# Running the first feed-forward chunks ahead of attention's last products

## The chip, the cores and the metric

The kernel runs on one core of one Trainium2 chip. The metric is the device time of one execution in microseconds (us). Before the change three runs gave 1016.50, 1019.47 and 1022.62 us, a median of 1019.47.

## What is computed

Three layers stand behind each other. Attention over 4 batches, 8 heads, 576 positions and head size 64 keeps only scores within `tau` of their row's largest. A dense layer `w_in`, `w_out` with a rational function in between (the "feed-forward part" below) takes its result. Last comes a mixture of 8 experts, one for each token.

```python
scores = scale * np.matmul(q, k.transpose(0, 1, 3, 2))
thresh = np.max(scores, axis=-1, keepdims=True) - tau
scores = np.where(scores >= thresh, scores, -1000000000.0)
attn = softmax(scores);  x = attn @ v            # (2304, 512) after the heads are put side by side
h = x @ w_in                                     # (2304, 2048)
g = (a0 + a1 h + a2 h^2 + a3 h^3) / (1 + |b0| |h| + |b1| h^2 + 1e-6)
x = g @ w_out                                    # (2304, 512)
e = argmax(x @ w_gate);  out = gate * sigmoid(x @ w_output_gate)[e] * (relu(x @ w1[e]) @ w2[e])
```

The products are made of two f16 (or rounded f32) parts of each number, a high part and a residue, so that three products stand for one in f32.

## The kernel before

**Attention** goes through 144 steps, one for 128 rows of scores; 18 steps make a pair of heads (group 0 to 7), two steps a pair that shares buffers. In step i TensorE makes the scores of step i + 1 (`emit_s`) and the products with v of step i - 12 (`emit_pv`), VectorE the row's extreme and the mask multiply (`emit_r`, `emit_p`: tiles `mn`, `e`), ScalarE the exponential and the f16 high part (`e`, `php`), GpSimd the residue (`php`, L382 and L388). For each pair SyncE's queue then transposes `php` into `pt`, from which the products with v are made. The scale of ring buffers lets the engines run some pairs ahead of the transposes. Every six steps VectorE normalises the products (`emit_x`: `rinv`, `xf`), which frees the bank for the next six; every eighteen, in three blocks of three token tiles, TensorE transposes x, ScalarE copies the high part into `xT` and VectorE subtracts for the residue (`emit_xt`, `emit_xlo`). The products of the last twelve steps come after step 143.

**The feed-forward part** is a generator, `moe1`, that issues one slot of work at each `next`. Attention calls it from step 112 on, so that slot t goes with step 112 + t; after slot 31 its buffers are opened, and what is behind slot END runs without attention. `w_in` and `w_out` come in 16 pieces each, of 128 columns or rows. The weights are read in 64-bit words, and a piece is decoded: ScalarE makes the exponent (L601), VectorE three operations (L598, L604, L608: `raw`, `mag`, `mag`). A piece of `w_in` is then summed on ScalarE (`sum_in`, L760), the sums of two pieces go through TensorE and VectorE's nine short operations to a scale (`red_in`, `clamp_red`, `scale_in`), and the piece is split: ScalarE scales it and writes the high part `wih` (L807, L808, or L810 for the later ones), GpSimd the residue `wil` (L812). A piece of `w_out` needs no scale (`split_out`: `woh` on ScalarE, `wol` on GpSimd). Pieces stand in the order `STREAM`; `FIRST_AT` gives the slots of the first eight decodes, `DEC_AT` and `DEC_EVERY` those of the others, `IN_LOAD` those of the first loads.

There are 96 **chunks**, each one piece of `w_in` times 384 tokens: twelve products into a bank of `h` (L900). Chunk c is issued in slot START + c, and the products with `w_out` of chunk c five slots later (`acc`, L969). Chunks 0 to 11 are pieces 0 to 3 for the first three blocks of tokens, which stem from head groups 0 to 3 and batches 0 and 1 alone; chunks 28 to 43 are pieces 0 to 15 for the sixth block. Two chunks, a pair, share the rational function. First half: ScalarE `ah`, `s`, `t` (L923 to L925), GpSimd `t` (L926), VectorE `s`, `s` (L928, L929). Second half, one pair later: ScalarE the logarithm and exponential (L935, L936) that give the quotient, VectorE `t`, `h`, `s` (L914 to L916), ScalarE `gh`, GpSimd `gl` (L951). There are two `h` buffers, so that chunk 4 can begin when VectorE has done L916 on pair 0, and chunk 6 when it has on pair 1. Every engine takes its instructions in the order in which they are issued.

Of the kernel before, what the change touches and what calls it, by code (L numbers as in the profile page):

```python
# [9 lines left out]
F32 = mybir.dt.float32  # L10
# [119 lines left out]
SUM_AT = (0, 1, 1, 2, 2)  # L130


def attention(nc, tc, q, k, v, tau, xT, vs, ident, tail):

# [6 lines left out]
    def pool(c, name, bufs, **kw):  # L141
        return c.enter_context(tc.tile_pool(name=name, bufs=bufs, side="right", reuse_waits="tile", **kw))
# [3 lines left out]
    pt_p = pool(ctx, "pt", 6)  # L146
    x_p = pool(ctx, "x", 2)
    ps_x = pool(ctx, "ps_x", 1, space=PSUM)
    raw_p = pool(early, "raw", 1)
    t_p = pool(early, "tt", 2)  # L150
    e_p = pool(early, "e", 3)
    ps_s = pool(early, "ps_s", 3, space=PSUM)

    D1 = D + 1
# [16 lines left out]
    tiny = fix.tile([P, P + 6 * D1], BF16, name="tiny")  # L171
    xps = ps_x.tile([P, 6, D1], F32, name="xps")
    xflat = xps.rearrange("p a b -> p (a b)")


    raws = {}
# [310 lines left out]
    def at(step, f, *a):  # L487
        plan.setdefault(step, []).append((f, a))
# [22 lines left out]
    for g in range(1, NG):  # L511
# [20 lines left out]
    pre = {min(6 * n + 6 + LAG, N + LAG - 1): n for n in range(N // 6)}  # L532
    for g in range(NG):
        for tg in range(3):
            s = (g + 1) * GT + PLAN["xt"][tg]
            if g == NG - 1:
                s = min(N + LAG - 1, N + 6 + 6 * tg)
            w = (g + 2, (("kt",), ("qt", 0), ("qt", 1))[tg]) if g + 2 < NG else ()
            at(s, emit_xt, g, tg, *w)
            at(s + 1, emit_xlo, g, tg)  # L540
    emit_s(0)
    i = 0
    while i < N + LAG or plan:
# [11 lines left out]
        if 0 <= i - 1 < N:  # L555
            emit_p(i - 1)
        if i < N:
            emit_thr(i)
        if i in pre and not done:
            emit_x(pre[i])  # L560
        while plan and min(plan) <= i:
            for f, a in plan.pop(min(plan)):
                f(*a)
        if i == N:
            early.close()
        if i >= N - PRE and tail:
            next(tail)
        i += 1
    ctx.close()


# [72 lines left out]
    return ((0, P, b0 + S + t - 5, 4),)  # L644


def moe1(nc, tc, xT, vs, w_in, w_out, a, bb, w_gate, w_ogate, gates, ident, yd, part, L, consts, keep, side):

    ctx, psum = ExitStack(), ExitStack()

# [18 lines left out]
    cvs = d_p.tile([P, 4, 2, NFC], F32, name="cvs")  # L669
    cv = cvs[:, 0]  # L670
    tot = d_p.tile([P, NFC], F32, name="tot")

    wo, ps_b, d2_p = [], [], []

# [62 lines left out]
        return p.tile([P, DM], F32, tag="mag", bufs=n, name="mag")  # L737

    def step(key):
        raw, t = raws[key], mags.pop(key, None)  # L740
        low, high = raw[:, :, 0], raw[:, :, 1]
        out = mags[key] = mag_buf(key[0])
        if t is not None:
            high = t.bitcast(I32)
            t = high
        elif late(key):
            t = aux().bitcast(I32)
            dec.last_bits(raw, t)
            low = t
        else:  # L750
            t = out.bitcast(I32)
            dec.last_bits(raw, low)
        dec.merge(t, high, low)
        dec.sign(out.bitcast(I32), raw[:, :, 1], t)
        del raws[key]
        load_next()

    def sum_in(n):

        nc.scalar.activation(  # L760
            wih[:, :, n * P:(n + 1) * P], mags[0, n].rearrange("p (k f) -> p k f", k=4), AF.Abs,
            accum_out=tot[:, n:n + 1])


# [10 lines left out]

    def red_in(n, m, alone=False):
        if alone:
            sum_rows(h_tile()[:, 0], n, tot[:, n:n + m], m)
        else:
            spare.append(lambda ps: sum_rows(ps, n, tot[:, n:n + m], m))  # L780

# [19 lines left out]
    def split_in(n):  # L801
        f = mags.pop((0, n)).rearrange("p (k f) -> p k f", k=4)
        sc = scales.pop(n)
        hi = wih[:, :, n * P:(n + 1) * P]
        lo = wil[:, :, n * P:(n + 1) * P]
# [14 lines left out]
    at(PRE, coefficients)  # L820
    end = decode_at()
    for key in STREAM:
        t = end[key]
        steps.setdefault(t, []).append(lambda key=key: step(key))
        at(t - SLOT_LEAD[late(key)], exponent, key)
        if late(key) and key[0]:
            at(t - SHIFT_LEAD, last_bits, key)
    n = 0
    for m in GROUPS:
        if n in FIRST_SUMS:  # L830
            t = FIRST_SUMS[n]
# [20 lines left out]
    for n in range(RAW_BUFS):  # L852
        at(IN_LOAD[n], load_next)
    for t in range(PRE):
        for f in chains(t):
            f()
        run(t)
        yield
    c_p = pool("c", 1)
    m_p = pool("m", 1)  # L860
    ps_h = pool("ps_h", 2, space=PSUM)
    ps_a = pool("ps_a", 1, space=PSUM)
    wih = c_p.tile([P, 4, FF], F16, name="wih")
    wil = c_p.tile([P, 4, FF], F16, name="wil")


    chunks = [(j, fc, r) for j, (r, (f0, f1), _) in enumerate(SEGS) for fc in range(f0, f1)]
# [20 lines left out]
    def emit_in(c, fill):  # L888
# [3 lines left out]
        if c < len(chunks):  # L892
            j, fc, r = chunks[c]
            t0 = TR * r
            if not odd:
                hps[p] = h_tile()
            hb = hps[p][:, odd]
            parts = [(wih, k, lo) for k in range(4) for lo in range(2)] + [(wil, k, 0) for k in range(4)]
            for i, (w, k, lo) in enumerate(parts):
                nc.tensor.matmul(  # L900
                    hb[:, 0:n], w[:, k, fc * P:(fc + 1) * P], xT[:, k, t0:t0 + TR, lo, :],
                    start=(i == 0), stop=(i == 11))
# [222 lines left out]
    for t in range(PRE, START + len(chunks) + G_LAG):  # L1125
# [18 lines left out]
        if t in hooks:  # L1144
            run(t)
        if t < END:
            yield
    assert not hooks, hooks
    ctx.close()
# [622 lines left out]
def kernel(ctx, tc, q, k, v, tau, w_in, w_out, a, b, w_gate, w_ogate, w1, w2, out):  # L1772
    nc = tc.nc
    with tc.manual_schedule():
# [20 lines left out]
        xT = mid.tile([P, 4, NTILE, 2, P], F16, name="xT")  # L1795
        masks.make_identity(nc, ident)
        experts = Experts(ctx, nc, tc, yd, L, rt, R, w1, w2, ident, out, xT)
        gen = moe1(nc, tc, xT, vs, w_in, w_out, a, b, w_gate, w_ogate, gates, ident, yd, part, L,
                   lambda tmp: routing_constants(nc, main, tmp, R), ctx, experts)
        attention(nc, tc, q, k, v, tau, xT, vs, ident, gen)  # L1800
        for _ in gen:
            pass
        experts.rest()
# [33 lines left out]
```

## Time and profile before

| | |
|---|---|
| median of three runs | 1019.47 us (1016.5 to 1022.62) |
| the profiled execution | 1021.39 us, of which the span of its instructions is 1019.7 |
| TensorE busy | 932.2 us, 91% of the span |
| VectorE busy | 795.7 us, 78% |
| ScalarE busy | 680.3 us, 67% |
| GpSimd busy | 543.6 us, 53% |
| mean granted clock of TensorE | 0.98 of full |

The busy shares are means over stages with different limits. By the order of time attention fills the span to about 300 us, the feed-forward part with its 96 chunks the stretch to some 755, the experts the rest. The rows below look at the end of attention, the change-over behind it, and the stretch in which the later pieces are decoded beside the chunks.

### The profile page before, as it was taken

The page shows a single profiled execution, that of the slowest core. Times are in us where ns is not written, and L with a number is a line of the kernel's source. Part 1 is how long each engine was busy: PE and PEld are TensorE (multiplying, and loading weights), DVE is VectorE, ACT ScalarE, POOL GpSimd, SP SyncE. Part 2 cuts the span into 40 slices and gives each one's busy share as a digit, 9 for nine tenths or more (in the row PEclk, how much of TensorE's full clock was granted, in tenths as well). Part 3 has the DMA queues.
Part 4 walks back from the last instruction along what each step waited for, and adds up shares of the span by engine and source line. Part 5 has one row for each costly group of instructions (what it writes and reads, how often), then busy time and mean ns, then how long its engine had stood idle before and what let it go on. Part 6 is the DMA issues. An engine that isn't in the chain of part 4 may idle for free.

```text
span 1019.7 us, 20739 instructions
## 1 busy us (share of the span) xinstructions
PE 932.2 (91%) x7899; PEld 683.6 (67%) x7899; DVE 795.7 (78%) x1337; ACT 680.3 (67%) x1006; POOL 543.6 (53%) x540
## 2 busy tenths in 40 slices
PE   8898899999876798999999899998798999999996
PEld 5565566666544465666666666665567899999995
DVE  5898799989896887888768878998983986555652
ACT  5888888888776677887866666656553555455551
POOL 2687689888774588697954344444241132111120
PEclk9999999999998899999999999999899999999998
DMA  9999999999994342232003212041123021111340
GB/s 215 176 208 203 199 190 182 184 196 185 215 196 126 103 143 96 82 114 73 1 1 94 73 53 63 32 106 60 42 52 134 22 63 42 42 42 42 119 130 24
DMA packets 234188, 110.26 MB, mean 108 GB/s; under 512 B 196832, under 2 KB 221408, under 8 KB 234080
## 3 DMA queue, kind: packets, MB, share of 16 engines
q1 hardware_dynamic: 230816, 98.89, 44.9%
q0 software_dynamic: 3120, 9.96, 3.0%
q8 instruction: 64, 1.05, 0.4%
q14 instruction: 44, 0.36, 0.1%
q10 hardware_dynamic: 144, 0.00, 0.0%
HBM read 82.61 MB, written 13.63 MB: 94 GB/s over the span
## 4 chain that ended last, share of the span: by engine, by line
PE 52%; DVE 20%; POOL 9%; issue 7%; ACT 6%; DMA 5%; SPq 0%; POOLq 0%; DVEq 0%; ACTq 0%
PE h L1638 10%; PE o L1655 9%; PE h L900 9%; PE acc L969 7%; PE s L352 5%; PE tp L202 5%; PE xps L410 4%; DMA pt<-php 4%; DVE t L914 2%; DVE h L915 2%; POOL t L926 2%; DVE s L916 2%; DVE s L928 2%; POOL php L382 2%; DVE s L929 2%
## 5 line engine op out<-in xcount | busy, mean ns | idle before, releaser
L382 POOL TENSOR_TENSOR php<-e,php 128x512 f16<-128x512 f32 x144 | 166.3, 1159 | 65.7 <-ACT php L380 65.2
L900 PE MATMUL h<-xT,wih 128*128 128x384 f16 x768 | 147.2, 336 | 37.7 <-DVE s L916 30.5
L926 POOL TENSOR_TENSOR t<-t,ah 128x768 f32<-128x768 f32 x48 | 87.8, 1829 | 167.1 <-ACT t L925 158.3
L900 PEld LDWEIGHTS <-wih 128*128 128x128 f16 x768 | 69.8, 100 | 103.9 <-DVE s L916 40.8
L969 PE MATMUL acc<-woh,gh 128*128 128x512 f32 x288 | 125.7, 437 | 1.1 <-ACT part L986 1.1
L364 ACT ACTIVATE e<-s,mn 128x576 f32<-128x576 f32 x144 | 107.0, 743 | 28.2 <-DVE mn L363 24.9
L376 DVE SCALAR_TENSOR_TENSOR e<-s,mn,e 128x576 f32<-128x576 f32 x144 | 116.4, 808 | 8.8 <-ACT e L364 8.8
L352 PE MATMUL s<-kt,qT 64*128 64x256 f32 (+3 forms) x640 | 115.6, 450 | 7.7 <-DVE mn L369 7.4
L1665 POOL DMA_INDIRECT out_dram<-os,sidx x19 | 23.6, 1243 | 184.3 <-ACT os L1664 154.3
L410 PEld LDWEIGHTS <-pt 128*128 128x128 f16 (+1 forms) x2240 | 78.2, 101 | 59.0 <-issue 55.9
L969 PE MATMUL acc<-woh,gl 128*128 128x512 f32 x288 | 114.0, 396 | 0.3 <-POOL gl L951 0.2
L969 PE MATMUL acc<-wol,gh 128*128 128x512 f32 x288 | 113.9, 396 | 0.0
L363 DVE TENSOR_REDUCE mn<-s 128x1 f32<-128x576 f32 x144 | 107.7, 748 | 6.8 <-PE s L352 6.5
L380 ACT ACTIVATE php<-e 128x576 f16<-128x576 f32 x144 | 98.6, 685 | 12.5 <-DMA pt<-php 11.1
L951 POOL TENSOR_TENSOR gl<-s,gh 128x768 fp32r<-128x768 f32 x48 | 91.4, 1904 | 5.7 <-issue 4.7
L410 PE MATMUL xps<-vs__112,pt 128*128 128x65 f16 (+1 forms) x2240 | 92.5, 195 | 0.0
L935 ACT ACTIVATE h<-t,co 128x768 f32<-128x768 f32 x48 | 43.5, 906 | 69.3 <-POOL t L926 28.6
L900 PE MATMUL h<-xT,wil 128*128 128x384 f16 x384 | 79.9, 332 | 0.0
L914 DVE SCALAR_TENSOR_TENSOR t<-t,co,h 128x768 f32<-128x768 f32 x48 | 48.5, 1011 | 34.7 <-POOL gl L951 22.6
L923 ACT ACTIVATE ah<-h,cvs 128x768 f32<-128x768 f32 x48 | 43.2, 901 | 42.0 <-PE h L900 37.0
L1598 DVE TENSOR_TENSOR wol<-xT,woh 128x1024 fp32r<-128x1024 f32 x45 | 56.8, 1271 | 13.5 <-ACT woh L1597 13.0
L969 PEld LDWEIGHTS acc<-woh,gh 128*128 128x128 f32 x288 | 54.5, 189 | 15.5 <-ACT part L986 2.2
(387 smaller groups left out, 2322.3 us busy)
## 6 DMA issues: line engine op xcount, KB each, us to landing
xT<-in_moe_w_dram SPq DMA_DIRECT2D x80, 512.0 KB
raw<-in_moe_w_in_dram SPq DMA_DIRECT2D x16, 512.0 KB
raw<-in_moe_w_out_dram SPq DMA_DIRECT2D x16, 512.0 KB
yd<-y SPq DMA_DIRECT2D x18, 256.0 KB
raw<-in_k_dram SPq DMA_DIRECT2D x16, 256.0 KB
raw<-in_q_dram SPq DMA_DIRECT2D x16, 256.0 KB
xT<-in_v_dram SPq DMA_DIRECT2D x8, 512.0 KB
part<-part SPq DMA_DIRECT2D x15, 256.0 KB
```

What stands on the lines that cost most here:

```text
L352: nc.tensor.matmul(ps[po:po + m, o:o + n], qT[r, g % 2, hh, t, po:po + m], KT[g][r, bb, c:c + n], start=True, stop=True)
L363: nc.vector.tensor_reduce(mn[:, n:n + 1], st[i], axis=AX.X, op=ALU.min)
L364: nc.scalar.activation(e[:, n], st[i], AF.Exp, bias=mn[:, n:n + 1], scale=-1.0)
L376: nc.vector.scalar_tensor_tensor(e[:, n], st.pop(i), mn[:, 2 + n:3 + n], e[:, n], op0=ALU.is_le, op1=ALU.mult)
L380: nc.scalar.activation(hi, e[:, n], AF.Copy)
L382: nc.gpsimd.tensor_tensor(lo[:, b:b + 512], e[:, n, a:a + 512], hi[:, a:a + 512], op=ALU.subtract)
L410: nc.tensor.matmul(x, pt[:, blk, po:po + m], vv[:, par, hh, j, :], start=False, stop=(i % 6 == 5 and n == 13))
L900: nc.tensor.matmul(hb[:, 0:n], w[:, k, fc * P:(fc + 1) * P], xT[:, k, t0:t0 + TR, lo, :], start=(i == 0), stop=(i == 11))
L926: nc.gpsimd.tensor_tensor(t1, t1, ah, op=ALU.mult)
L969: nc.tensor.matmul(acc[r, i], g[:, i * P:(i + 1) * P], w, start=first and m == 0, stop=last and m == 2)
L1638: self.nc.tensor.matmul(hp[:, a], w[:, k, a], x[:, k], start=(k == 0 and m == 0), stop=(k == K1 - 1 and m == 2))
L1655: self.nc.tensor.matmul(self.Op[j][h], a[:, k, h * P:(h + 1) * P], w[:, k], start=(u == 0 and k == 0 and m == 0), stop=(u == UN - 1 and k ...
```

## The change

Pieces 0 and 1 of `w_in` are decoded and split within attention: the three operations of VectorE on a decode are issued in steps 121, 123, 125 and 127, 129, 131 (`EARLY_STEPS`), the sums in steps 126 and 132, the scale in step 133, the splits in steps 135 and 137. The first four pieces get a buffer of their own, `w4`, that exists from the start, and the buffers for decoded pieces go from 6 to 4 in one pool and from 4 to 6 in the other. The first loads come in steps 112, 115, 125, 129 and 133, not 112, 114, 118, 122 and 127. START goes from 44 to 33, END from 45 to 37, DEC_AT from 48 to 39. After step 143 attention no longer runs its loop on, but calls the generator between its last products: chunks 0 and 1, products of steps 132 to 137, the sums of pieces 2 and 3, products of steps 138 to 141, chunk 2, products of steps 142 and 143, chunk 3, the last two blocks of x.

```diff
-MAG_BUFS = 6
-MAG2_BUFS = 4
+MAG_BUFS = 4
+MAG2_BUFS = 6
-END = 45
-START = 44
+END = 37
+START = 33
-IN_LOAD = (0, 2, 6, 10, 15, 18, 20, 26)
+IN_LOAD = (0, 3, 13, 17, 21, 32, 32)
+EARLY_STEPS = ((9, 11, 13), (15, 17, 19))
+EARLY_SUM = 20
-FIRST_AT = (32, 33, 38, 42, 44, 45, 46, 47)
+FIRST_AT = (13, 19, 32, 33, 35, 37, 37, 38)
-FIRST_SUMS = {0: 41, 2: 43}
-DEC_AT = 48
+SECOND_SUM = 34
+HALVES = (34,)
+DEC_AT = 39
...
+    next(tail)
+    next(tail)
+    for i in range(N - LAG, N - 6):
+        emit_pv(i)
+    next(tail)
+    emit_x(N // 6 - 2)
+    for i in range(N - 6, N - 4):
+        emit_pv(i)
+    next(tail)
+    for i in range(N - 4, N - 2):
+        emit_pv(i)
+    emit_xt(NG - 1, 0)
+    emit_xlo(NG - 1, 0)
+    next(tail)
+    for i in range(N - 2, N):
+        emit_pv(i)
+    emit_x(N // 6 - 1)
+    next(tail)
+    for tg in (1, 2):
+        emit_xt(NG - 1, tg)
...
+    w4 = [d_p.tile([P, 4, 4 * P], F16, name=x) for x in ("wih4", "wil4")]
...
+        if n < 2 * m:
             for i in range(n, n + m):
-                at(end[0, i], sum_in, i)
-                at(t + 1, split_in, i)
-            at(t, red_in, n, m, True)
-            at(t, clamp_red, n, m)
-            at(t, scale_in, n, m)
-            at(t + 2, factors_in, n, m)
+                at(end[0, i] + (n == 0), sum_in, i)
+            t = SECOND_SUM if n else EARLY_SUM + 1
+            at(t + 0.5, red_in, n, m, True)
+            at(t + 0.75, clamp_red, n, m)
+            at(t + 0.75, scale_in, n, m)
+            for i in range(m):
+                at(t + (0.8, 1)[i] if n else t + 2 + 2 * i, split_in, n + i)
+            at(t + 1, factors_in, n, m)
```

GpSimd's list at the end of attention was, from step 134 on (`php`: the residues of a pair of steps):

```order
L333 TENSOR_TENSOR vs__112<-vt,vs__112 128x2x2x64
L382 TENSOR_TENSOR php<-e,php 128x512
L388 TENSOR_TENSOR php<-e,php 128x2x64
L382 TENSOR_TENSOR php<-e,php 128x512 x2
L388 TENSOR_TENSOR php<-e,php 128x2x64
```

and is now, with `cvs` the factors and `wil` the residues of pieces 0 and 1:

```order
L337 TENSOR_TENSOR vs__112<-vt,vs__112 128x2x2x64
L386 TENSOR_TENSOR php<-e,php 128x512
L392 TENSOR_TENSOR php<-e,php 128x2x64
L835 TENSOR_TENSOR cvs<-sc,vs 128x2x2
L838 TENSOR_TENSOR cvs<-cvs 128x2x2
L840 TENSOR_SCALAR cvs<-cvs,co 128x2x2 x2
L386 TENSOR_TENSOR php<-e,php 128x512
L852 TENSOR_TENSOR wil_4009<-mag,wih_4008 128x4x128
L386 TENSOR_TENSOR php<-e,php 128x512
L392 TENSOR_TENSOR php<-e,php 128x2x64
```

Four operations on columns and a residue of a weight piece stand between the residues of attention; a second residue follows in the next pair.

VectorE's list behind attention's last mask multiply was, at its start:

```order
L376 SCALAR_TENSOR_TENSOR e<-s,mn,e 128x576
L598 TENSOR_SCALAR raw<-raw 128x512
L604 SCALAR_TENSOR_TENSOR mag<-raw 128x512
L608 SCALAR_TENSOR_TENSOR mag<-raw,mag 128x512
```

and is now:

```order
L380 SCALAR_TENSOR_TENSOR e<-s,mn,e 128x576
L451 TENSOR_TENSOR xT<-tp,xT 128x3x128
L619 TENSOR_SCALAR raw<-raw 128x512
L625 SCALAR_TENSOR_TENSOR mag<-raw 128x512
L629 SCALAR_TENSOR_TENSOR mag<-raw,mag 128x512
L619 TENSOR_SCALAR raw<-raw 128x512
L625 SCALAR_TENSOR_TENSOR mag<-raw 128x512
L629 SCALAR_TENSOR_TENSOR mag<-raw,mag 128x512
L975 SCALAR_TENSOR_TENSOR s<-s,cvs,h 128x768
L976 SCALAR_TENSOR_TENSOR s<-s,cvs,h 128x768
L424 RECIPROCAL rinv<-xps 128x6
L425 TENSOR_TENSOR xf<-xps,rinv 128x384
```

The decodes are now those of pieces 2 and 3, the first half of chunks 0 and 1 (L975, L976) comes next, and the normalising of steps 132 to 137 behind it.

## Rows read from the trace of the kernel before

**Rows 1.** Busy us by stretch: start:end, length, each engine (instructions), PEclk, DMA share, GB/s.
```profile
255.00:298.00 43.00, 35.20 (x536) 23.12 (x535) 38.34 (x79) 33.99 (x59) 35.50 (x45) 1.00 1.12 203
...
317.38:345.66 28.28, 18.15 (x82) 9.88 (x82) 23.88 (x37) 20.55 (x30) 20.21 (x19) 0.77 0.34 99
345.66:506.72 161.06, 150.75 (x768) 100.33 (x769) 135.24 (x209) 128.53 (x186) 129.42 (x106) 1.00 0.26 84
```

**Rows 2.** SyncE's queue: start, us, queue, line, transfer, count.
```profile
249.23 3.62 SPq L390 DMA_TRANSPOSE pt<-php  x1
...
288.52 18.40 SPq L390 DMA_TRANSPOSE pt<-php  x6
```

**Rows 3.** VectorE's instructions: start, us, line, out<-in; in brackets idling before, releaser.
```profile
263.17 0.82 DVE L376 SCALAR_TENSOR_TENSOR e<-s,mn,e 128x576 f32<-128x576 f32 x1 [2.22 <-ACT e L364]
...
271.59 0.82 DVE L376 SCALAR_TENSOR_TENSOR e<-s,mn,e 128x576 f32<-128x576 f32 x1 [1.40 <-ACT e L364]
...
297.83 0.81 DVE L376 SCALAR_TENSOR_TENSOR e<-s,mn,e 128x576 f32<-128x576 f32 x1
298.55 1.03 DVE L598 TENSOR_SCALAR raw<-raw 128x512 int32<-128x512 int32 x1
...
301.24 0.80 DVE L608 SCALAR_TENSOR_TENSOR mag<-raw,mag 128x512 int32<-128x512 int32 x1
...
302.05 0.42 DVE L598 TENSOR_SCALAR raw<-raw 128x512 int32<-128x512 int32 x1
...
303.30 0.69 DVE L608 SCALAR_TENSOR_TENSOR mag<-raw,mag 128x512 int32<-128x512 int32 x1
...
305.63 0.18 DVE L420 RECIPROCAL rinv<-xps 128x6 f32<-128x6 f32 x1
305.85 0.56 DVE L421 TENSOR_TENSOR xf<-xps,rinv 128x384 f32<-128x384 f32 x1
```

**Rows 4.** TensorE's instructions at the change-over: chunks 4, 6 and 8 begin.
```profile
308.99 2.27 PE L410 MATMUL xps<-vs__112,pt 128*64 128x65 f16 x56
...
334.93 2.74 PE L900 MATMUL h<-xT,wih 128*128 128x384 f16 x8 [8.29 <-DVE s L916]
...
345.66 1.47 PE L900 MATMUL h<-xT,wih 128*128 128x384 f16 x8 [1.84 <-DVE s L916]
...
354.75 1.47 PE L900 MATMUL h<-xT,wih 128*128 128x384 f16 x8 [0.82 <-DVE s L916]
```

**Rows 5.** ScalarE's instructions: copy of x, a split, first half of a pair, logarithm.
```profile
304.66 0.47 ACT L441 ACTIVATE xT<-tp 128x384 f16<-128x384 f32 x1
...
315.27 0.70 ACT L807 ACTIVATE mag<-mag,sc 128x512 f32<-128x512 f32 x1
316.01 0.63 ACT L808 ACTIVATE wih<-mag 128x512 f16<-128x512 f32 x1
...
322.83 0.90 ACT L923 ACTIVATE ah<-h,cvs 128x768 f32<-128x768 f32 x1 [0.50 <-PE h L900]
...
327.46 0.91 ACT L935 ACTIVATE h<-t,co 128x768 f32<-128x768 f32 x1 [0.85 <-POOL t L926]
```

**Rows 6.** VectorE's instructions on pair 0, and a decode between.
```profile
324.65 1.01 DVE L928 SCALAR_TENSOR_TENSOR s<-s,cvs,h 128x768 f32<-128x768 f32 x1 [3.43 <-ACT s L924]
...
326.70 1.01 DVE L598 TENSOR_SCALAR raw<-raw 128x512 int32<-128x512 int32 x1
...
331.81 1.01 DVE L914 SCALAR_TENSOR_TENSOR t<-t,co,h 128x768 f32<-128x768 f32 x1
...
333.85 1.01 DVE L916 SCALAR_TENSOR_TENSOR s<-s,co,h 128x768 f32<-128x768 f32 x1
```

**Rows 7.** TensorE: end of chunk 39, start of chunk 40, and chunk 84.
```profile
495.34 0.81 PE L900 MATMUL h<-xT,wil 128*128 128x384 f16 x4
...
498.34 1.47 PE L900 MATMUL h<-xT,wih 128*128 128x384 f16 x8
...
692.24 2.74 PE L900 MATMUL h<-xT,wih 128*128 128x384 f16 x8 [2.20 <-DVE s L916]
```

**Rows 8.** GpSimd: the residue of piece 14 of w_in.
```profile
503.64 1.16 POOL L812 TENSOR_TENSOR wil<-mag,wih 128x512 f16<-128x512 f32 x1
```

More of the change, by code (lines that the diff above doesn't have):

```diff
@@ L130, with attention @@
 SUM_AT = (0, 1, 1, 2, 2)
-def attention(nc, tc, q, k, v, tau, xT, vs, ident, tail):
+def attention(nc, tc, q, k, v, tau, xT, vs, ident, tail, bank):
     ctx = ExitStack()
@@ L148, in attention @@
     ps_x = pool(ctx, "ps_x", 1, space=PSUM)
+    e_p = pool(early, "e", 3)
+    t_p = pool(early, "tt", 2)
     raw_p = pool(early, "raw", 1)
-    t_p = pool(early, "tt", 2)
-    e_p = pool(early, "e", 3)
     ps_s = pool(early, "ps_s", 3, space=PSUM)
@@ L173, in attention @@
     xflat = xps.rearrange("p a b -> p (a b)")
+    bank.append(lambda: ps_x.tile([P, 4, P], F32, tag="tp", name="tp")[:, 3])
     raws = {}
@@ L531, in attention @@
             at(s0 + s, lo_v, g, a)
-    pre = {min(6 * n + 6 + LAG, N + LAG - 1): n for n in range(N // 6)}
+    pre = {6 * n + 6 + LAG: n for n in range(N // 6 - 2)}
     for g in range(NG):
         for tg in range(3):
-            s = (g + 1) * GT + PLAN["xt"][tg]
+            s = min((g + 1) * GT + PLAN["xt"][tg], N)
             if g == NG - 1:
-                s = min(N + LAG - 1, N + 6 + 6 * tg)
+                continue
             w = (g + 2, (("kt",), ("qt", 0), ("qt", 1))[tg]) if g + 2 < NG else ()
             at(s, emit_xt, g, tg, *w)
-            at(s + 1, emit_xlo, g, tg)
+            at(min(s + 1, N), emit_xlo, g, tg)
     emit_s(0)
-    i = 0
-    while i < N + LAG or plan:
+    for i in range(N + 1):
         if i + 1 < N:
             emit_s(i + 1)
-        done = i in pre and i < N + LAG - 1
-        if done:
+        if i in pre:
             emit_x(pre[i])
-        if 0 <= i - LAG < N:
+        if LAG <= i < N:
             emit_pv(i - LAG)
@@ L554, in attention @@
             emit_r(i)
-        if 0 <= i - 1 < N:
+        if i > 0:
             emit_p(i - 1)
@@ L558, in attention @@
             emit_thr(i)
[L559 to L563, printed above, removed]
+        for f, a in plan.pop(i, ()):
+            f(*a)
         if i == N:
             early.close()
-        if i >= N - PRE and tail:
+        if i >= N - PRE:
             next(tail)
-        i += 1
+    assert not plan, plan
+    next(tail)
[18 more added lines that the diff above has]
+        emit_xt(NG - 1, tg)
+    for tg in (1, 2):
+        emit_xlo(NG - 1, tg)
     ctx.close()
@@ L644, in rows_of, with moe1 @@
     return ((0, P, b0 + S + t - 5, 4),)
-def moe1(nc, tc, xT, vs, w_in, w_out, a, bb, w_gate, w_ogate, gates, ident, yd, part, L, consts, keep, side):
+def moe1(nc, tc, xT, vs, w_in, w_out, a, bb, w_gate, w_ogate, gates, ident, yd, part, L, consts, keep, side, early_bank):
     ctx, psum = ExitStack(), ExitStack()
@@ L739, in step, with step_parts, bits, merge @@
     def step(key):
[L740 to L756, printed above, removed]
+        for part in step_parts(key):
+            part()
+    def step_parts(key):
+        now = {}
+        def bits():
+            raw, t = raws[key], mags.pop(key, None)
+            low, high = raw[:, :, 0], raw[:, :, 1]
+            out = mags[key] = mag_buf(key[0])
+            if t is not None:
+                high = t.bitcast(I32)
+                t = high
+            elif late(key):
+                t = aux().bitcast(I32)
+                dec.last_bits(raw, t)
+                low = t
+            else:
+                t = out.bitcast(I32)
+                dec.last_bits(raw, low)
+            now.update(t=t, high=high, low=low, out=out)
+        def merge():
+            dec.merge(now["t"], now["high"], now["low"])
+        def sign():
+            dec.sign(now["out"].bitcast(I32), raws.pop(key)[:, :, 1], now["t"])
+            if key not in STREAM[:2]:
+                load_next()
+        return bits, merge, sign
     def sum_in(n):
         nc.scalar.activation(
-            wih[:, :, n * P:(n + 1) * P], mags[0, n].rearrange("p (k f) -> p k f", k=4), AF.Abs,
+            w_cols(0, n), mags[0, n].rearrange("p (k f) -> p k f", k=4), AF.Abs,
             accum_out=tot[:, n:n + 1])
@@ L818, in split_out @@
         nc.gpsimd.tensor_tensor(l, f, h.bitcast(F32), op=ALU.subtract)
-    at(PRE, coefficients)
+    at(1, coefficients)
     end = decode_at()
@@ L823, in moe1 @@
         t = end[key]
-        steps.setdefault(t, []).append(lambda key=key: step(key))
+        if key in STREAM[:2]:
+            for x, f in zip(EARLY_STEPS[STREAM.index(key)], step_parts(key)):
+                steps.setdefault(x, []).append(f)
+            t = EARLY_STEPS[STREAM.index(key)][0]
+        else:
+            steps.setdefault(t, []).append(lambda key=key: step(key))
         at(t - SLOT_LEAD[late(key)], exponent, key)
@@ L851, in moe1 @@
     queue = list(STREAM)
-    for n in range(RAW_BUFS):
-        at(IN_LOAD[n], load_next)
+    for t in IN_LOAD:
+        at(t, load_next)
     for t in range(PRE):
@@ L856, in moe1 @@
             f()
-        run(t)
+        for x in (t, t + 0.5, t + 0.75):
+            run(x)
         yield
+    m_p = pool("m", 1)
     c_p = pool("c", 1)
-    m_p = pool("m", 1)
     ps_h = pool("ps_h", 2, space=PSUM)
     ps_a = pool("ps_a", 1, space=PSUM)
-    wih = c_p.tile([P, 4, FF], F16, name="wih")
-    wil = c_p.tile([P, 4, FF], F16, name="wil")
+    wih = c_p.tile([P, 4, FF - 4 * P], F16, name="wih")
+    wil = c_p.tile([P, 4, FF - 4 * P], F16, name="wil")
     chunks = [(j, fc, r) for j, (r, (f0, f1), _) in enumerate(SEGS) for fc in range(f0, f1)]
@@ L1146, in moe1 @@
         if t < END:
+            yield
+        for x in ((0.5,), (0.75, 0.8)) if t in HALVES else ():
+            for y in x:
+                run(t + y)
             yield
```

20 lines of the change are left out of this document (11 added, 9 removed).

## The prediction

> **What bounds the kernel now.** I read the busy time by stretch first, then the engines' lists of instructions around the end of attention, then the same lists around chunk 42, whose weights the change also moves. In the last 43 us of attention VectorE is busy 38.34 us and GpSimd 35.50, 83% [rows 1]; SyncE's queue moves one transpose after the other, the last six alone from 288.52 to 306.92 [rows 2]. So two limits lie close together there: the transposes and VectorE, and where VectorE stops it is for the transposes, 2.22 and 1.40 us at ScalarE [rows 3]. Then comes the change-over. VectorE's last mask multiply of attention ends at 298.64 (297.83 + 0.81) [rows 3]; TensorE's chunk 4 begins at 334.93 after 8.29 us of idling, chunk 6 at 345.66 and chunk 8 at 354.75, each released by VectorE's last operation on an earlier pair of chunks [rows 4]. Between chunks 0 and 6 TensorE works 18.15 of 28.28 us, at a mean granted clock of 0.77 [rows 1], so part of that stretch runs at the lower of its levels (1.2 of 2.4 GHz). After it TensorE is the bound: chunks 6 to 42 take 161.06 us with 150.75 busy, at clock 1.00 [rows 1]. Time is to be won between 298.64 and 354.75, 56.1 us, by giving VectorE less there; whatever delays TensorE after that is lost one to one.
>
> **A. Attention's last 32 steps get longer: +5.1 us.** Two decodes, two exponents, two sums, two splits, the coefficients and one set of nine scale operations move in between. VectorE: a decode took 3.5 us while GpSimd worked (298.55 to 302.04) and 1.9 alone (302.05 to 303.99) [rows 3]. With GpSimd busy 83% that is 0.83 x 3.5 + 0.17 x 1.9 = 3.2 each, 6.4 for two. Nine scale operations and three for the coefficients are short ones on one or two columns, estimated at 0.1 each, 1.2. ScalarE's two splits (0.70 + 0.63 each [rows 5]) stand between an exponential and the next; of their 2.7 us I put 1.1 on VectorE, between nothing (ScalarE has 9 us of idling in those 43 [rows 1]) and all. Sum 8.7. Against it stand the 3.6 us in which VectorE waits now [rows 3]: three of the five weight loads come later in SyncE's queue, the transposes before them earlier, and I count the whole of it as cover. 8.7 - 3.6 = 5.1. The lower end is 0 (decodes of 1.9, no split on VectorE: 5.0, less 3.6 and a little more that the earlier transposes give), the upper 11 (7.0 + 1.2 + 2.7, nothing covered). The GpSimd work (two residues of some 1.2 us, four column operations) fits its idle 17%, 7.5 us; if it doesn't, the last transpose is late, and that is not needed before the products of the last two steps, some 17 us after zero below. The transposes' total is unchanged, five loads before and after.
>
> The trace shows a decode's first operation at 1.03 us beside GpSimd and 0.42 without [rows 3]. The Trainium skill ("SBUF — State Buffer", SBUF: two separate sides) says that such an operation and a GpSimd one hold a shared pair of ports in turn, the second waiting for the whole of the first. The row agrees in kind; taken strictly, GpSimd too would stop for each of the six moved operations, and the sum for A would go to its upper end.
>
> **B. From the last mask multiply to chunk 8: 46.3 us instead of 56.1, -9.8.** Chunks 0 and 1 now stand right behind the transposes of the last x block of head pair 6, ahead of the last twelve steps' products. I follow VectorE's list with the durations of before, from zero at the end of the mask multiply. It waits for ScalarE's copy of that block and subtracts: 1.6 (some 0.6 for the last f16 copy, 0.47 [rows 5], 0.5). Decodes of the third and fourth piece: 2.4 (GpSimd still busy for half of it) and 1.9, to 5.9. ScalarE's sum 0.7, then its two operations on chunks 0 and 1, 1.8 (322.83 to 324.65 [rows 5, 6]), to 8.4. VectorE's two on them 2.05 (324.65 to 326.70 [rows 6]), and only behind these the normalising of steps 132 to 137, 0.8 with the 0.56 of its product [rows 3]: 11.25. TensorE has finished its products by then and waits for this; 56 products with v 2.3 [rows 4], about 1.2 lost to the clock after the idling, as below, the x transposes 0.8: 15.6. ScalarE's queue then holds a copy 0.47, the logarithm 0.91 and an exponential like it [rows 5], two exponents of some 0.65, and the fourth piece's split 1.3: 20.2. Chunk 3, 2.0: 22.2. ScalarE on chunks 2 and 3 1.8, VectorE 2.05: 26.1. Two more copies on ScalarE keep VectorE until 27.1; with its subtractions 28.0. Two decodes beside GpSimd 5.1 (326.70 to 331.81) and the second half of pair 1, 3.05 (331.81 to 334.86) [rows 6]: 36.1, where chunk 6 begins. A decode of 2.9, 2.05, a decode of 2.1, 3.05: 46.3, chunk 8. Six decodes on that path make 14.4; all alone they would be 11.4, all beside GpSimd 21. So B lies between -12.8 and -3.2, and I stay with -9.8, since GpSimd's list is full in the second half only. A and B bring chunk 8 forward by 4.7 us.
>
> **C. The later decodes stand two chunks later, +0.7.** Chunks 0 to 5 are eleven slots earlier, the decodes from the ninth piece on nine. Chunks 8 to 42 will carry the decodes that chunks 6 to 40 carry now: 152.68 (345.66 to 498.34) instead of 151.97 (354.75 to 506.72) [rows 1, 4, 7]. Bounds 0 and, for one decode on TensorE's path, 3.5.
>
> **D. Chunk 42 must wait for its weights, +5.6.** It is the first that multiplies with piece 14 of w_in. Now that piece's split is issued behind chunk 39: chunk 39 ends at 496.15, the residue on GpSimd at 504.80 (503.64 + 1.16), 8.65 later [rows 7, 8], because the pair's two GpSimd products go before it. Chunk 42 begins at 506.72 [rows 1]. Two chunks later the same split stands behind chunk 41, while a chunk starts 2.19 after the end of the one before (496.15 to 498.34) and takes some 2.1 (1.47 and 0.81, overlapping [rows 7]). Its last four products can now begin 8.65 after, and end some 0.7 later: 9.3 instead of 4.3, 5.0 lost, with TensorE the bound and nothing beside it. After such a wait the clock may fall: behind 2.20 us of idling the eight products that take 1.47 took 2.74 [rows 7]; I take half of this 1.3. Nothing of it is lost if ScalarE and GpSimd run ahead of TensorE by 5 us there, which these rows exclude unless TensorE is held up just before; then part of it would fall on a wait that is there anyway. Bounds 0 and 7.
>
> The first output products, with their weight pieces split only four chunks in, come some 2 us after chunk 5, but chunk 6 waits for VectorE longer than that: nothing. The other pieces keep 10 us or more. The smaller buffers (four instead of six for decoded pieces) are each free before they are taken again: nothing, unless the order slips by four pieces.
>
> **Sum.** +5.1 - 9.8 + 0.7 + 5.6 = +1.6. The profiled execution took 1021.39 us (span 1019.7); so 1023.0 on its scale. It is 1.9 above the median of the runs, 1019.47; against the median that makes 1021.1, and I predict 1021.
>
> **Rivals.** *The change-over wins more and attention pays less* (faster). If the moved operations hide in VectorE's waits (A near 1) and the decodes run alone (B -12.8), the sum is +1 - 12.8 + 0.7 + 5.6 = -5.5, 1014; without the wait at chunk 42, 1008. For it: VectorE waited 3.6 us in that stretch, and GpSimd has nothing after attention's last residue for some 15 us now. Against it: nearly full engines before 298, and a list for VectorE after it that is still serial.
> *VectorE and GpSimd block each other throughout* (slower). The place is steps 121 to 131 and the decodes after chunk 3; the price is 3.5 us for each decode: A +8 (7.0 + 1.2 + 2.7 - 3.6 = 7.3, and some on GpSimd's side), B -5, C and D as above: +9.3, 1029. It decides once A + B is above about -1. For it: 1.03 against 0.42 us in the row. Against: after 302 the same operations ran alone.
> *The early chunks are only issued early* (slower a little). The sums of the third and fourth piece and the first chunks' work stand ahead of the normalising on ScalarE and VectorE, so that TensorE idles there instead; then A + B is 0 and C and D remain: +6.3, 1026. For it: the 4 us of idling in my own chain at 11. Against: VectorE has two decodes fewer after zero.
>
> **How the numbers follow.** A measurement here tells about 0.5%, 5.1 us, from no change; so faster is below 1014.4, slower above 1024.6. The likeliest case (1016 to 1024.6 alone) has 0.45. The first rival 0.28, faster. The second 0.19 and the third 0.08, slower, 0.27 together. For 8 in 10 the range has to take in part of both sides: from 1012, where the first rival keeps its wait at chunk 42, to 1028, just short of the second. It leaves out the first rival without that wait and the worse half of the second.
>
> **What would show it.** Right: VectorE's last mask multiply at 303 to 305 instead of 298.64; chunk 6 some 36 us and chunk 8 some 46 us behind it; a wait of TensorE at chunk 42 on GpSimd's residue, 5 us in one or two pieces, perhaps with the lower clock behind it. Wrong: the mask multiply at 300 (A), chunk 8 before 345 or after 353 (B), chunk 42 without a wait (D), or new waits between chunks 8 and 40 (C).

## The result, and the profile after

The changed kernel takes 1032.61 us in the median (1028.72 to 1033.16, four runs), the kernel before 1019.09 beside it: a ratio of 1.0122, 95% interval 1.0083 to 1.0162. Slower by some 12 us; 1021 was predicted, with 1028 as the upper end. The profiled execution took 1033.16 us, span 1031.4, mean clock 0.975.

Where the 11.7 us of span are is found by cutting both traces at the same instructions. The first mark is the start of ScalarE's copy to f16 (`php`) that is the 35th from the last, in a step ahead of every edit; the second the end of the last mask multiply; then the starts of chunks 8, 40 and 44.

| stretch, us | before | after | difference | forecast |
|---|---|---|---|---|
| start to the first mark | 234.07 | 235.28 | +1.2 | - |
| A: to the end of the last mask multiply | 64.57 | 77.05 | +12.5 | +5.1 |
| B: to chunk 8 | 56.11 | 49.09 | -7.0 | -9.8 |
| C: chunk 8 to 40 | 143.59 | 143.60 | 0.0 | +0.7 |
| D: chunk 40 to 44 | 16.48 | 21.65 | +5.2 | +5.6 |
| chunk 44 to the end | 504.86 | 504.71 | -0.1 | - |

One term is far off, A, and the list of VectorE around step 113 of attention shows why (start, us, line, out<-in; in brackets the idle time before it and what ended it):

```profile
239.46 0.81 DVE L380 SCALAR_TENSOR_TENSOR e<-s,mn,e 128x576 f32<-128x576 f32 x1
...
249.80 0.17 DVE L682 TENSOR_SCALAR co<-co 128x4 f32<-128x4 f32 x1 [9.41 <-DMA co<-in_moe_a_dram]
...
311.52 0.81 DVE L380 SCALAR_TENSOR_TENSOR e<-s,mn,e 128x576 f32<-128x576 f32 x1
```

A 0.17 us operation, the negation of the coefficients a, stands in VectorE's list behind 9.41 us of nothing. The change moved it: the line `at(PRE, coefficients)`, step 144, became `at(1, coefficients)`, step 113. ScalarE waits in the same step for b, and the two engines behind them wait for these:

```profile
250.73 0.48 PE L404 MATMUL xps<-tiny 128*128 128x390 bf16 x1 [9.10 <-DVE xf L425]
...
250.81 0.20 ACT L683 ACTIVATE co<-co 128x2 f32<-128x2 f32 x1 [9.35 <-DMA co<-in_moe_b_dram]
...
252.86 1.16 POOL L386 TENSOR_TENSOR php<-e,php 128x512 f16<-128x512 f32 x1 [9.14 <-ACT php L384]
```

All four engines lose the same 9 us, so nothing runs that could make it up. The loads themselves are on SyncE's queue:

```profile
238.78 4.25 SPq L394 DMA_TRANSPOSE pt<-php  x1
...
243.81 3.17 SPq L394 DMA_TRANSPOSE pt<-php  x1
247.03 0.57 SPq L678 DMA_DIRECT2D co<-in_moe_a_dram  x1
...
254.43 2.68 SPq L394 DMA_TRANSPOSE pt<-php  x1
```

They are written down in step 112, right ahead of the coefficients; but SyncE is behind VectorE there, since the transposes that stand before them hold its queue, 4.25 and 3.17 us for the last two; how much of such a time is waiting for a residue and how much the issue itself, the profile does not part. It comes to the load of a at 247.03, 6.8 us after VectorE's mask multiply of that step has ended, and the data takes 2.8 us more. Behind it the next transpose, 254.43, waits for a mask that the standing engines have not made.

The last stretch of attention answers to the first of [rows 1]: VectorE now has next to no room left. Its 42.97 of 43.70 us are 98%, where it was 38.34 of 43.00, 89%.

```profile
265.40:309.10 43.70, 37.03 (x550) 24.45 (x550) 42.97 (x92) 37.49 (x66) 39.16 (x49) 1.00 0.96 180
```

TensorE at the change-over (to be held against [rows 4]) and at chunk 42:

```profile
323.25 0.48 PE L404 MATMUL xps<-tiny 128*128 128x390 bf16 x1 [4.08 <-DVE xf L425]
...
333.30 1.47 PE L947 MATMUL h<-xT,wih 128*128 128x384 f16 x8 [1.69 <-ACT wih L848]
...
350.89 2.72 PE L947 MATMUL h<-xT,wih 128*128 128x384 f16 x8 [3.92 <-DVE s L963]
...
510.38 0.81 PE L947 MATMUL h<-xT,wil 128*128 128x384 f16 x4
...
516.02 2.74 PE L947 MATMUL h<-xT,wih 128*128 128x384 f16 x8 [2.74 <-ACT wih L850]
...
519.85 0.82 PE L947 MATMUL h<-xT,wil 128*128 128x384 f16 x4 [1.08 <-POOL wil L852]
```

The one wait of 8.29 us ahead of chunk 4 has become several short ones, and chunk 6 begins (350.89) 38.6 us behind the mask multiply. The last three rows are term D: chunk 41 ends at 511.19 (510.38 + 0.81), chunk 42 waits 2.74 us for the high part of piece 14 and 1.08 for its residue, and its first eight products take 2.74 us instead of 1.47.

### The profile page after: what moved, and what is told of

It is laid out like the page before. It is cut to its first block, busy times and chain, and to the rows that moved or that the text cites. A ratio compares the mean times of both kernels' runs of the same rounds, so it can differ in the third digit from the quotient of the medians.

```text
span 1031.4 us, 20730 instructions
## 1 busy us (share of the span) xinstructions
PE 934.7 (91%) x7899; PEld 685.4 (66%) x7899; DVE 797.6 (77%) x1337; ACT 680.4 (66%) x1006; POOL 542.5 (53%) x540
## 5 line engine op out<-in xcount | busy, mean ns | idle before, releaser
L947 PE MATMUL h<-xT,wih 128*128 128x384 f16 x768 | 145.0, 333 | 34.5 <-DVE s L963 22.4
L970 ACT ACTIVATE ah<-h,cvs 128x768 f32<-128x768 f32 x48 | 43.3, 903 | 47.9 <-PE h L947 43.4
```

What stands on the lines that cost most here:

```text
L947: nc.tensor.matmul(hb[:, 0:n], w_cols(w, fc)[:, k], xT[:, k, t0:t0 + TR, lo, :], start=(i == 0), stop=(i == 11))
```

## The experiments

All ratios are to the kernel before, run on the same chip. The stretches are those of the table above, from one profile each. Runs 1 to 4, 5 to 8, 9 and 10, 11 and 12 stand beside the same runs of the kernel before; runs 6 to 8 are edits of run 5's kernel. The expectations from the sixth on count B from the start of the last mask multiply, 0.8 us earlier, and the fifth, ninth and eleventh D to chunk 43.

| edit | ratio, 95% | A | B | C | D | 44 to 95 |
|---|---|---|---|---|---|---|
| before | 1 | 64.6 | 56.1 | 143.6 | 16.5 | 237.4 |
| the change | 1.0122 (1.0083 to 1.0162) | 77.1 | 49.1 | 143.6 | 21.7 | 237.2 |
| 1 coefficients later | 1.0003 (0.9981 to 1.0026) | 68.0 | 48.8 | 143.5 | 21.6 | 237.1 |
| 2 loads on ScalarE's queue | 1.0049 (1.0027 to 1.0071) | 71.0 | 49.1 | 143.5 | 21.7 | 237.9 |
| 3 before, coefficients early | 1.0086 (1.0056 to 1.0116) | 70.9 | 58.3 | 143.5 | 16.5 | 238.3 |
| 4 decodes denser | 1.0077 (1.0050 to 1.0105) | 77.2 | 49.2 | 146.1 | 16.5 | 234.3 |
| 5 = 1, pieces swapped | 0.9988 (0.9967 to 1.0009) | 68.1 | 48.9 | 143.8 | 20.0 | 236.7 |
| 6 = 5, chunks not between | 1.0078 (1.0053 to 1.0103) | 65.6 | 55.2 | 143.9 | 20.1 | 238.2 |
| 7 = 5, decode in the gap | 0.9981 (0.9964 to 0.9999) | 65.6 | 51.1 | 143.9 | 20.1 | 233.3 |
| 8 = 5, half of the early decodes | 0.9966 (0.9946 to 0.9985) | 65.7 | 49.8 | 143.5 | 20.0 | 239.7 |
| 9 = 1 + 4 | 0.9997 (0.9979 to 1.0015) | 65.7 | 48.9 | 146.1 | 16.5 | 239.8 |
| 10 = 9, gap, exponent later | 0.9920 (0.9893 to 0.9947) | 67.1 | 45.3 | 146.4 | 16.5 | 237.1 |
| 11 = 10, one slot earlier | 0.9964 (0.9948 to 0.9981) | 65.6 | 47.9 | 143.2 | 18.9 | 234.8 |
| 12 = 11, scale later | 0.9959 (0.9935 to 0.9984) | 67.3 | 48.6 | 143.7 | 18.9 | 237.1 |

**1. The coefficients later.**

```diff
-    at(1, coefficients)
+    at(10, coefficients)
```

> The changed kernel with one number altered: the coefficients' operations (VectorE negates a, ScalarE takes |b|) are issued in slot 10 instead of slot 1, still ahead of their first use in slot 21; loads and all else stay. Theory (wait): the 9.41 us for which VectorE idled at 249.80 for the load of a are lost by all engines, and nothing else late takes their place, since both loads have landed by 250.6. The last mask multiply ends near 303 instead of 312.25, the distance from there to chunk 8 stays 49, and the time is 1032.6 - 9.4 = 1023 us (1022 to 1025). Rival (shared work): the attention is longer because the decodes and the early products take VectorE's and TensorE's time; the wait only stood where these would have cost it anyhow: the last mask multiply stays above 309 and the time above 1029.

Measured 1022.04 us. A falls by 9.0 us and B, C and D stay within 0.3; VectorE's and ScalarE's operations on a and b (259.79 and 260.89) wait for nothing, with the loads issued at 248.82 and 249.44. The theory holds, the rival falls.

**2. The loads on another queue.**

```diff
-    nc.sync.dma_start(out=co[:, 0:4], in_=a.to_broadcast([P, 4]))
-    nc.sync.dma_start(out=co[:, 8:10], in_=bb.to_broadcast([P, 2]))
+    nc.scalar.dma_start(out=co[:, 0:4], in_=a.to_broadcast([P, 4]))
+    nc.scalar.dma_start(out=co[:, 8:10], in_=bb.to_broadcast([P, 2]))
```

> The changed kernel with the two loads of a and b issued by ScalarE instead of SyncE; the coefficients stay in slot 1. Theory (queue): the loads were late because SyncE issues them in order behind transposes that wait for their masks (issued at 247.03 and 247.65, landed 2.8 us later). From ScalarE they are issued at about 240 and have landed near 243, so VectorE's wait shrinks from 9.4 to 2 or 3 us and the time is 1032.6 - 7 = 1026 (1024 to 1027.5). Rival (load itself): small loads of this kind take that long by themselves at this place, from whatever queue: the wait stays above 7 us and the time above 1030.

Measured 1027.64 us, a ratio 0.0073 below the change's. ScalarE issues the load of a at 239.51, and VectorE's wait is

```profile
244.56 0.17 DVE L682 TENSOR_SCALAR co<-co 128x4 f32<-128x4 f32 x1 [3.46 <-DMA co<-in_moe_a_dram]
```

instead of 9.41. The load takes longer than I expected (5.0 us from issue to the end of the wait; 2.8 on SyncE's queue), but most of the wait was the place in SyncE's queue: 5.95 of the 9.41 us are gone, and A is 6.0 shorter. The time is 0.1 us above what the theory allowed, and the rival falls.

**3. That part alone, in the kernel before.**

```diff
-    at(PRE, coefficients)
+    at(1, coefficients)
```

> The kernel before with that one part of the change alone: the coefficients in slot 1 instead of slot 32; no early decode, no early chunks. Theory (wait): VectorE and ScalarE wait some 9 us in step 113 here too, the last mask multiply moves from 298.64 to about 307.5, and the time is 1019.1 + 9 = 1028 (1026 to 1029.5). Rival (shared work): alone, the wait is taken up by slack between the engines: under 1022.

Measured 1031.19 us, 1.0086: by itself, without one early decode or chunk, this line costs 8.8 us (5.7 to 11.9). VectorE waits 8.11 us in step 113. Of it 6.3 are left at the last mask multiply, since the waits of 2.22 and 1.40 us in [rows 3] are gone in this profile; B is 2.2 longer, at a mean granted clock of 0.79 instead of 0.85. The two directions give 9.0 us (run 1, A) and 8.8 (here, the time). By the time, run 1 gives 12, but with some 5 us of uncertainty, from the two intervals.

**4. Chunk 42's wait.**

```diff
-DEC_EVERY = 1.6
+DEC_EVERY = 1.5
```

> The changed kernel with the later decodes 1.5 slots apart instead of 1.6, so that piece 14 of w_in is split two chunks earlier; the coefficients stay in slot 1. Theory: chunk 42's wait of 2.74 us, its wait of 1.08 and the half clock of 2.74 us behind them go (5.2 in all); the denser decodes cost under 1 us: 1032.6 - 5 = 1027.5 (1026.5 to 1029). Rival: with decodes closer together VectorE falls behind by as much in chunks 8 to 41, and the wait only moves: 1031 or more. The wait for a and b stays at 9.4 us in both.

Measured 1029.39 us. D is gone to the last tenth (16.49, before 16.48), so its size was 5.2. But chunks 8 to 40 take 2.5 us longer with the denser decodes, the rival's mechanism at half its size: ahead of chunk 38 TensorE now has two waits, 0.96 us for GpSimd at 496.47 and the one below (from chunk 37 to 38 6.9 us, with the change 4.1; the time from 44 to 95, where nothing was edited, is 2.9 us shorter than with the change):

```profile
499.63 1.48 PE L947 MATMUL h<-xT,wih 128*128 128x384 f16 x8 [1.26 <-DVE s L963]
```

**5. Both mended, the second by a swap** of two pairs in the list of pieces.

```diff
-... (0, 12), (0, 13), (1, 10), (1, 11), (0, 14), (0, 15), ...
+... (0, 12), (0, 13), (0, 14), (0, 15), (1, 10), (1, 11), ...
```

> The coefficients in slot 10 as in the first run, and in the list of pieces (0,14) and (0,15) stand ahead of (1,10) and (1,11), so that piece 14 of w_in is decoded and split three slots earlier and nothing else of the list moves. Theory: both late items are gone: the wait for a and b (9 us), and chunk 42's wait with the half clock behind it (5.2 us: from chunk 40 to 43 12.4 us instead of 17.6). Pieces (1,10) and (1,11) are still in time. Against the kernel before that makes 1.0003 - 0.0051 = 0.995 of its time, some 5 us less; what is left of the change then is the attention longer by 3.4 and the change-over shorter by 7. Rival: one more late item takes the place of chunk 42 (the pieces of w_out that were pushed back): a ratio of 0.999 or more.

Measured 1020.68 us, 0.9988: not distinguishable from the kernel before, as the rival said. Chunk 42 no longer waits for piece 14, but of D's 5.2 us only 1.6 are gone. It waits for VectorE instead, as chunk 44 does at 514.53, and VectorE had idled for GpSimd:

```profile
501.23 1.01 DVE L961 SCALAR_TENSOR_TENSOR t<-t,co,h 128x768 f32<-128x768 f32 x1 [3.49 <-POOL gl L998]
```

```profile
504.35 1.47 PE L947 MATMUL h<-xT,wih 128*128 128x384 f16 x8 [1.26 <-DVE s L963]
```

GpSimd has hardly a gap from 483.68 to 511.33. The decodes of two w_out pieces that VectorE now does beside chunk 42 (504.20 and 507.51) come behind this wait; which of GpSimd's operations would have to move, no run shows.

**6. The early chunks' work behind attention's last products.** All six calls that issue it in attention's closing part stand at its end.

```diff
-    next(tail)
...
     for tg in (1, 2):
         emit_xlo(NG - 1, tg)
+    next(tail)
+    next(tail)
+    ...
```

> The kernel of the run before this (coefficients in slot 10, the two pieces swapped) with the work of slots 32 to 36, chunks 0 to 3 among it, issued behind attention's last products with v and its last transposes instead of between them. Theory (the early chunks fill time in which TensorE would wait): from the last mask multiply to chunk 8 it takes 53 to 56 us instead of 49.7 (before: 56.9), and the time is 3 to 6 us above that kernel. Rival (the early chunks are only issued early; chunk 8 is set by the decodes on VectorE): from mask multiply to chunk 8 it stays within 1 us of 49.7, and so does the time.

Measured 1028.97 us, 8 us above the fifth. B is 55.2, 6.3 longer and nearly what it was before the change. So the interleaving itself is what shortens the change-over; my third rival (the early chunks are only issued early) is out.

**7. A decode in VectorE's gap.**

```diff
-FIRST_AT = (13, 19, 32, 33, 35, 37, 37, 38)
+FIRST_AT = (13, 19, 32, 33, 34, 35, 37, 38)
...
+        elif key == (1, 0):
+            at(t + 0.9, step, key)
```

> The same kernel as the first of this call, with the decode of piece (1,0) moved into the 4.95 us for which VectorE waits for ScalarE's copy of xT, and the decode of (1,1) into the place that (1,0) had. Theory: chunk 6 waits 3.58 us for a product s that stands on VectorE behind the two decodes (1,1) and (1,2), which take 6.9 us beside GpSimd, and then runs at half clock (2.72 instead of 1.47); with one decode less ahead of it the wait and the half clock go: 3.5 us less (2.5 to 4.8). Rival: the decode in the gap outlasts the copy that it hides behind, and the exponent of (1,0) that moves ahead of ScalarE's sums makes TensorE wait longer there: within 1 us of the first.

Measured 1019.48 us; B grew by 2.3 us. Chunk 6 waits only 0.74 us, as hoped (its eight products still take 2.72), but ScalarE was handed the exponent of (1,1) two slots earlier, ahead of a sum that the chunks wait for, and its load had not landed:

```profile
312.25 0.65 ACT L622 ACTIVATE raw<-raw 128x512 f32<-128x512 f32 x1 [6.73 <-DMA raw<-in_moe_w_out_dram]
```

TensorE's wait for that sum went from 1.04 to 7.24 us. The time is the rival's; the exponent that made TensorE wait is that of (1,1), not of (1,0). It is the mistake of the coefficients once more, made by me.

**8. Two of three operations of each early decode left out.**

```diff
-                dec.last_bits(raw, low)
+                low = high if key in STREAM[:2] else dec.last_bits(raw, low) or low
...
-            dec.sign(now["out"].bitcast(I32), raws.pop(key)[:, :, 1], now["t"])
+            raw = raws.pop(key)
+            if key not in STREAM[:2]:
+                dec.sign(now["out"].bitcast(I32), raw[:, :, 1], now["t"])
```

> The first kernel of this call with two of the three VectorE operations left out of each of the two decodes within attention (the last bits and the sign are not computed, the merge stays), four operations of 0.70 and 0.95 us, 3.3 us in all. Theory: the 3.4 us by which attention's end is later once the wait for a and b is gone are these operations' own time on VectorE, which paces attention's steps: attention's end comes 3 us earlier and so does the end of all (2.3 to 3.4). Rival: they fit into VectorE's idle time and attention is later because ScalarE or TensorE do more there: under 1 us.

Measured 1018.79 us, A 65.7. The runs with all operations have A from 65.6 to 68.1 with the same instructions (runs 1, 5, 6, 7, 9, 10 and 11). Much of that spread is one wait of ScalarE, for a transpose, here in runs 1, 7 and 8:

```profile
263.82 0.68 ACT L384 ACTIVATE php<-e 128x576 f16<-128x576 f32 x1 [2.09 <-DMA pt<-php]
```

```profile
260.86 0.69 ACT L384 ACTIVATE php<-e 128x576 f16<-128x576 f32 x1 [0.68 <-DMA pt<-php]
```

```profile
262.65 0.68 ACT L384 ACTIVATE php<-e 128x576 f16<-128x576 f32 x1 [2.02 <-DMA pt<-php]
```

Where it is under 1 us (runs 6, 7, 9 and 11), A is 65.6 or 65.7; in runs 1 and 5, with 2.09 and 1.74, A is 68.0 and 68.1. (Run 10 has no such wait and 67.1; its mean granted clock in A is 0.95, that of runs 6, 7 and 11 is 1.00, that of run 9 0.97.) Run 8 has the wait of 2.02 and still 65.7: against runs 1 and 5 the operations left out are worth 2.4 us, against the others nothing. Over A VectorE is busy 61.25 us in run 8 and 63.11 in run 7, and idles 4.45 instead of 2.51: between these two the work taken from it came back as waiting. The 3 us that I expected don't show.

**9. The first and the fourth edit together.**

> The coefficients in slot 10 and the later decodes 1.5 slots apart, pieces in their old order: the two edits that took 12 us and 5 us off the changed kernel, together. Theory (the two late items are separate and add): from chunk 40 to 43 12.4 us, VectorE's wait for a and b gone, a ratio of 1.0122 - 0.0119 - 0.0045 = 0.996 of the kernel before (0.994 to 0.998). Rival (as with the swapped pieces, the gain at chunk 42 is given back by other operations of the denser decodes): 0.999 or more.

Measured 1022.63 us, 0.9997: not below the first alone. The trace has the wait and D gone (A 65.7, D 16.5), C 2.5 longer, and from chunk 44 to 95, where nothing was edited, 239.8 us instead of 237.2. In these fourteen profiles that stretch lies anywhere from 233.3 to 239.8, and it hides a difference of 2 or 3 us. The granted clock is part of it, 0.99 in the shortest (run 7) and 0.97 in the two longest (runs 8 and 9); run 4 has 234.3 at 0.98 and the kernel before 237.4, so the rest is open.

**10. The seventh edit with its flaw taken out, on the ninth.**

```diff
-        at(t - SLOT_LEAD[late(key)], exponent, key)
+        at(t - 0.1 if key == (1, 1) else t - SLOT_LEAD[late(key)], exponent, key)
```

> The kernel of the run before this with the decode of (1,0) in VectorE's gap and that of (1,1) in its old place, as tried before, but with the exponent of (1,1) issued on ScalarE behind the split of piece 2 instead of ahead of the sum of piece 1, where it waited 6.73 us for its load. Theory (an in-order engine was handed an operation whose load had not landed): TensorE's wait of 7.24 us for the sum is back at 1.0 us, chunk 6's wait stays under 1 us instead of 3.6, and from the last mask multiply to chunk 8 it takes 46 us (45 to 47) instead of 49.7: 3.5 us below the run before this. Rival: the load of (1,1) lands too late for its new place as well, and another engine waits for it: 49 us or more.

Measured 1014.70 us against 1022.68 of the kernel before, 0.9920 (0.9893 to 0.9947): the fastest of all, 8 us below the kernel before and some 20 below the change. The median is 7.9 us below the ninth's, where 3.5 were forecast; of the difference 2.7 stand in the profiles from chunk 44 to 95, which the edit doesn't touch. B is 45.3, 3.6 less, as forecast:

```profile
336.65 1.46 PE L949 MATMUL h<-xT,wih 128*128 128x384 f16 x8 [1.39 <-DVE s L965]
```

This is chunk 6: a wait of 1.39 instead of 3.92 us with the change (somewhat more than the 1 I allowed), and 1.46 instead of 2.72 for its products. The wait for the sum is 1.04 again.

**11. All later decodes one slot earlier, spacing 1.6.**

```diff
-DEC_AT = 39
-DEC_EVERY = 1.5
+DEC_AT = 38
+DEC_EVERY = 1.6
```

> The fastest kernel so far (coefficients in slot 10, the decode in the gap, the exponent of (1,1) behind the split), with all later decodes one slot earlier and 1.6 slots apart instead of 1.5 apart. Theory (chunk 42's wait of 2.74 us is shorter than a slot, so one slot is enough, and the spacing of 1.6 does not crowd VectorE): from chunk 8 to 40 144 us instead of 146.3, from chunk 40 to 43 12.4 to 13, so 2.3 us less than the run before: a ratio near 0.990. Rival: what was gained at chunk 42 is given back wherever the decodes go: the two stretches together stay within 1 us of 158.8.

Measured 1018.42 us, 0.9964. Chunks 8 to 43 take 3 us less, as the theory had it, but one decode more now falls ahead of chunk 8, which waits 4.93 us for VectorE instead of 2.21 (B 47.9, 2.6 more), and from chunk 43 to 44 it takes 6.3 us instead of 4.1. Up to chunk 44, A left out, that is 1.8 us more than in the tenth: what is taken from one place turns up in the next.

**12. The scale one step later.**

```diff
-            at(t + 0.75, scale_in, n, m)
+            at(t + (0.75 if n else 1.5), scale_in, n, m)
```

(and the clamp and factors that go with it)

> The kernel before this with the scale of pieces 0 and 1 worked out by VectorE one step of attention later (slot 22.5 instead of 21.75), so that TensorE's sum has ended when VectorE comes to it. Theory (of what the change still costs within attention, some 2 us come in the step in which VectorE waits 0.59 us for that sum, and ScalarE, GpSimd and the transposes behind it start late): 0.6 to 2 us less up to the last mask multiply. Rival: the nine small operations cost their 0.8 us wherever they stand, and the wait of 0.59 us is all there is to gain: 0.6 us or less, not seen in the time.

Measured 1017.97 us, A 67.3. VectorE no longer waits for the sum, and the two steps around it take 3.83 us (mask multiplies at 282.61 and 286.44) instead of 4.51 in the eleventh: 0.7 less in its own place. But ScalarE has its wait for a transpose in this profile, 2.15 us, which the eleventh has not, so that A is longer, and in the time no gain is seen. That is the lower end of the theory and nearly the rival's number; the two are not told apart.

## Why the prediction was wrong

**The step that failed is in A:** "Nine scale operations and three for the coefficients are short ones on one or two columns, estimated at 0.1 each, 1.2." The three were priced as work (0.06 to 0.17 us each, so that was near enough) and not as a wait. Moved from behind attention to step 113 they come one step after their loads are written down. The trace of before had the answer: there too SyncE comes to these loads late,

```profile
246.37 0.57 SPq L657 DMA_DIRECT2D co<-in_moe_a_dram  x1
```

while VectorE's mask multiply of step 112 ends at 239.05 (238.24 + 0.81). Those are 7 us, and the landing comes on top. I read SyncE's queue only for how three weight loads would delay the transposes [rows 2], not for who waits on what stands in it. By their stretches runs 1 (A) and 3 (A and B) put the price at 9.0 and 8.5 us; with 9 the sum of +1.6 becomes +10.6, and the time 1030, against a measured 1032.61.

**The rest of A** was +1.0 to +3.5 us (seven profiles, against one of the kernel before) for a forecast of +5.1. A decode within attention took 2.5 us (0.69, 0.87 and 0.95), not 3.2. VectorE is busy 63.11 of 65.62 us in run 7's A, and 58.16 of 64.57 before: some 5 us of work instead of the 8.7 forecast, of which its old waits cover 3.9, near the 3.6 that I counted. Where A is longer than in run 7, most of it goes with ScalarE's wait for a transpose (see run 8). The rule that I set beside [rows 3], from the Trainium skill ("SBUF — State Buffer", SBUF: two separate sides), that one engine waits for the whole of the other's operation, agrees with this trace at the change-over: the last operation of a decode takes 2.19 us (345.68) while GpSimd is in one of 2.21 (345.11), and 0.69 alone:

```profile
345.68 2.19 DVE L629 SCALAR_TENSOR_TENSOR mag<-raw,mag 128x512 int32<-128x512 int32 x1
```

```profile
345.11 2.21 POOL L973 TENSOR_TENSOR t<-t,ah 128x768 f32<-128x768 f32 x1 [1.08 <-ACT t L972]
```

Within attention the same operation took 0.95, beside GpSimd operations of 1.2 us or less, and GpSimd's next one took 0.88 (275.82) instead of 0.43. Both engines lose some time there, but A stayed far from the upper end that I had tied to the rule.

**B** was -7.0 for -9.8. The chain was right up to chunk 3 (21.0 us behind the mask multiply, forecast 20.2; the terms of that step add up to 20.5). Of the 2.0 that it then lost most is one pair of decodes, 7.0 us (340.87 to 347.87) instead of 5.1, beside three GpSimd operations of 1.80, 1.51 and 2.21 us. Run 10 shows the size of that place: with one decode less in it B is 45.3.

**C** was 0.0 for +0.7. **D** was right in place, cause and size: 5.2 for 5.6. The last four products of chunk 42 begin 8.66 us (519.85) behind the end of chunk 41, with 8.65 forecast, and they wait for the residue. Not forecast was that the high part comes late too, 2.74 us; that wait and the slower products fall into the same 8.66, so the half of 1.3 for the clock was not lost. Run 4 takes D away. Of the rivals, the first had B at -12.8 and D's wait as the only loss; the second had 3.5 us for each decode in attention, which took 2.5, so that its 1029 comes near the measured time by luck, without the wait that made it; the third falls with run 6.

The change was right in its idea and lost by two late items: without them it is level with the kernel before (run 9, 0.9997), and 8 us faster only when the decodes of the change-over are moved as well (run 10). Whether D is better mended as in run 4 or left as it is, these runs don't tell: by the traces the denser decodes win 5.2 and give back 2.5.

## What to carry to other kernels

An operation that moves to an earlier place takes its inputs' arrival with it: before pricing its duration, look up on the issuing queue when the load that it reads is reached (not where it is written), and what the in-order engine has behind it. A 0.2 us operation cost 9 us here, and an exponent that was moved in run 7 made TensorE wait 6 us longer in the same way. In a pipeline where TensorE is the bound and the three other engines are at 80 to 84% (the last of [rows 1]), a decode taken from one chunk must be followed to the chunk where it lands.

## What the runs showed that I had not expected

The same load of 128 x 4 values took 2.8 us from issue to the end of the wait on SyncE's queue and 5.0 on ScalarE's, where it was issued at 239.51 instead of 247.03; whether the queue or the moment makes the difference, no run shows. And equal instruction lists gave A anything from 65.6 to 68.1 us, the start of attention anything from 233.78 to 237.09, and chunks 44 to 95 from 233.3 to 239.8: runs of the kernel before lie between 1016.50 and 1026.04, so a gain of 2 us is to be read in its own stretch of the trace, not in the total, and there only against a profile with the same waits.
